# Cosine attention, Fourier mixing and a feed-forward layer on one core: pairs of tiles that cross batches, scoring groups of three, and a new table of priorities

## The chip, the cores and the metric

The kernel runs on one core of one Trainium2 chip. The metric is the device time of one execution in microseconds (us), as the median of the runs shown. The core has five engines with an instruction stream each: TensorE (PE, matmuls; its weight loads are listed apart as PEld), VectorE (DVE), ScalarE (ACT), GpSimd (POOL) and SyncE (SP, which issues most DMAs).

## What is computed

Eight batches, 12 heads, 448 positions, head size 64; D = 768. Inputs and output are float32.

```python
q_n = q / (norm(q) + 1e-6);  k_n = k / (norm(k) + 1e-6)
attn = softmax(q_n @ k_n.T / tau)          # tau = 0.1
x = attn @ v                               # heads side by side: (8, 448, 768)
u = x + real(fft(fft(x, axis=1), axis=2))
un = (u - mean(u)) / sqrt(var(u) + 1e-6)   # over the 768 features
out = u + relu(un @ w_ch1) @ w_ch2         # 768 -> 3072 -> 768
```

## The kernel before

**Stages.** Each batch passes through three. `attn` (line 907) normalizes queries and keys on ACT, DVE and POOL, transposes them by DMA on SP, scores them on PE (line 973 for the three full key tiles of 128, line 986 for the 64 keys that are left, called the tail), takes exponentials on ACT (line 951) and multiplies with the values on PE (lines 1004 and 1010). It does so for six head pairs, called positions. `fft` (line 1165) makes the two transforms as matmuls with cosine and sine matrices; the last of them, over columns, are line 1191. DVE then adds the parts (line 1222), forms u (line 1233) and takes the mean (line 1270). ACT takes the variance and 1/sqrt (lines 1275 and 1278), DVE writes the normalized tile (line 1282, `un`), and SP transposes it by DMA into the buffer UNT (line 1303, `tru`). `ffn` (line 1558) runs the two feed-forward layers.

**Tiles of rows.** The 448 rows of two batches are seven tiles of 128: an even batch has three, an odd one four. A feed-forward unit is one tile or a pair. Which are pairs is set by `units` (line 1322) and by the loop in `ffn` (line 1601): a batch with three tiles has one pair and one lone tile, the lone tile first in batches 0 and 6 and last in 2 and 4; a batch with four has two pairs.

**First layer** (`up`, matmul at line 1350): 24 blocks of 128 hidden features, 6 matmuls each, 144 in all, with 256 columns for a pair and 128 for a lone tile. Pairs of batches 6 and 7 use `ups` (line 1445), a scheme with fewer products that needs sums of weights (DVE, lines 1387 to 1430). The weights of the first layer are in W1b.

**Second layer** (`prod`, matmul at line 1494, always 12 to a product, 384 columns): a lone tile takes 4 products on the weights W2b. A pair takes 7 products by Strassen's scheme: the hidden tiles in the buffer HQ are combined by DVE (`comb`, line 1593: 6 combinations, 3 of them of a third of the length), some products use precomputed sums of weights in the buffer TX, and three products are copied out by ACT (line 1514) and completed by POOL (line 1519). `fin` (lines 1508 to 1530) adds u and `store` (line 1535) writes the rows out.

**Scoring.** PSUM has two pools of buffers, 2 single banks ("M", for feed-forward) and 3 double banks ("G", for scores, values and transforms). One key tile of one position fills a double bank. Which key tiles are scored in one go is the list `steps` (line 958): batch 0 one at a time, batches 1 to 3 two at a time, batches 4 to 7 three at a time:

```python
elif b >= 4:
    steps = [[(pos, kt) for kt in range(3)]]
else:
    steps = [[(pos, 0), (pos, 1)], [(pos, 2), (pos + 1, 0)]] if pos % 2 == 0 else [[(pos, 1), (pos, 2)]]
```

In batches 4 to 7 each key tile of a head is scored by two matmuls (of 128 and 97 columns) per half of the queries, in batches up to 3 by one of 225.

**What sets the order of the work.** The program is a list of operations with inputs, buffers and a priority. A planner (line 257) simulates the five engines with a table of durations and, at each engine, issues the ready operation with the lowest priority number; the result is a fixed instruction order per engine. Second and first layers have priority numbers of 5000 and more, so that they fill what attention and transforms leave free. The table SHIFT (line 80) adds a number to the priority of single operations by name. Where the planner still sees PE idle, filler matmuls are put in (line 1737).

Of the kernel before, what the change touches and what calls it, by code (L numbers as in the profile page):

```python
# [25 lines left out]
TF = 4  # L26
ORDER = (0, 1, 2, 3, 5, 4)
# [473 lines left out]
class Kern:  # L501
# [405 lines left out]
    def attn(self, b):  # L907
# [890 lines left out]
```

## Time and profile before

| | |
|---|---|
| median of 3 runs | 578.84 us (578.64 to 579.3) |
| span of the profiled execution | 575.2 us |
| busy: PE, DVE, ACT, POOL | 97%, 75%, 67%, 38% of the span |
| DMA | 62.20 MB, mean 108 GB/s |
| granted TensorE clock | 9 tenths or more in all 40 slices |

The span is the time from the first to the last instruction that the profiler recorded in one execution; the time of a run is taken outside it and is longer by what lies around the span. The page gives the span of the profiled execution and no other time of it. Busy time is a sum over instructions of one engine. In timelines the matmuls of a run overlap by the depth of PE's pipeline, so a row's length is a little more than the distance from its start to the start of the next row.

### The profile page before, as it was taken

The numbers are of one execution on the slowest core, as the hardware profiler recorded it, in microseconds if no ns is written. First come the engines' busy times: TensorE is split into PE (matmuls) and PEld (weight loads), VectorE is DVE, ScalarE is ACT, GpSimd is POOL, SyncE is SP. The second block draws the span as 40 slices with busy tenths as digits, with TensorE's granted clock in tenths as the row PEclk, the third lists the DMA queues.
The fourth block names the chain that finished last, engine by engine and source line by source line (L and its number), as shares of the span: only waits on it lengthen the run. The fifth ranks groups of instructions, "written<-read, shape, count | busy, mean of one in ns | idle before, by whom it ended". The sixth has DMA issues, their size and how long they took to land.

```text
span 575.2 us, 16313 instructions
## 1 busy us (share of the span) xinstructions
PE 555.8 (97%) x6766; PEld 436.2 (76%) x6766; DVE 430.6 (75%) x917; ACT 385.3 (67%) x724; POOL 220.3 (38%) x332
## 2 busy tenths in 40 slices
PE   3899999999999999999999999999999999989997
PEld 3569787676787686878788787778778787959694
DVE  8989968996669869975669669776778579986262
ACT  7898885564876885687558875577637853747270
POOL 7534414356329544612370724523270210041303
PEclk9999999999999999999999999999999999999999
DMA  9999999975459739952595429743591210023001
GB/s 188 224 233 171 166 186 130 171 152 111 111 94 103 178 76 135 142 127 62 112 121 93 102 80 147 150 84 85 89 113 29 43 57 28 2 43 72 28 28 56
DMA packets 187898, 62.20 MB, mean 108 GB/s; under 512 B 166800, under 2 KB 185616, under 8 KB 187824
## 3 DMA queue, kind: packets, MB, share of 16 engines
q1 hardware_dynamic: 129856, 38.35, 33.7%
q0 software_dynamic: 57968, 22.81, 30.9%
q8 instruction: 53, 0.87, 0.6%
q14 instruction: 21, 0.17, 0.1%
HBM read 51.90 MB, written 11.01 MB: 109 GB/s over the span
## 4 chain that ended last, share of the span: by engine, by line
PE 60%; DVE 4%; ACT 2%; issue 0%; DVEq 0%; ACTq 0%
PE PS L1494 23%; PE PS L1350 20%; PE PS L1445 6%; PE PS L1010 4%; PE PS L973 3%; DVE U L1233 1%; PE PS L1004 1%; PE PS L986 1%; ACT E L951 1%; DVE ACG L1222 1%; ACT F L1275 1%; PE PS L1134 1%; PE PS L1191 1%; DVE SM L885 1%; DVE HQ L1593 1%
## 5 line engine op out<-in xcount | busy, mean ns | idle before, releaser
L1350 PE MATMUL PS<-UNT,W1b 128*128 128x256 bf16 (+1 forms) x1872 | 186.1, 256 | 1.2 <-DMA UNT<-F 0.6
L1350 PEld LDWEIGHTS PS<-UNT,W1b 128*128 128x128 bf16 x1872 | 155.5, 98 | 20.1 <-issue 2.7
L951 ACT ACTIVATE E<-PS 128x900 bf16<-128x900 f32 (+1 forms) x192 | 148.0, 827 | 19.1 <-PE PS L973 16.6
L1494 PE MATMUL PS<-W2b,HQ 128*128 128x384 bf16 x768 | 133.1, 326 | 0.0
L896 POOL TENSOR_TENSOR QH<-STG,SM 128x256 bf16<-128x256 f32 x126 | 82.3, 679 | 91.9 <-DVE SM L702 73.3
L1494 PEld LDWEIGHTS PS<-W2b,HQ 128*128 128x128 bf16 x768 | 73.3, 98 | 46.2 <-issue 0.7
L1519 POOL TENSOR_TENSOR OUTB<-OUTB,U 128x192 f32<-128x192 f32 x66 | 43.2, 675 | 138.5 <-ACT OUTB L1514 137.3
L1366 ACT ACTIVATE HQ<-PS 128x512 bf16<-128x512 f32 x81 | 48.2, 595 | 40.0 <-PE PS L1350 39.5
L1494 PE MATMUL PS<-TX,HQ 128*128 128x384 bf16 (+2 forms) x408 | 69.7, 321 | 1.8 <-ACT MV L1278 1.6
L883 ACT ACTIVATE QH<-STG 128x384 f32<-128x384 f32 x84 | 42.7, 520 | 25.8 <-DVE SM L885 21.3
L1494 PEld LDWEIGHTS PS<-TX,HQ 128*128 128x128 bf16 x408 | 38.4, 98 | 25.7 <-ACT MV L1278 2.0
L1593 DVE TENSOR_TENSOR HQ<-HQ 128x1536 bf16<-128x1536 bf16 (+1 forms) x69 | 49.5, 721 | 9.9 <-ACT HQ L1366 7.1
L885 DVE TENSOR_REDUCE SM<-QH 128x6 f32<-128x384 f32 x84 | 44.7, 544 | 11.3 <-ACT QH L883 11.0
L1010 PE MATMUL PS<-VB,E 128*128 128x65 bf16 x1152 | 51.4, 193 | 0.0
L1366 DVE TENSOR_SCALAR HQ<-PS 128x512 bf16<-128x512 f32 x45 | 31.0, 688 | 23.8 <-PE PS L1350 23.4
L1010 PEld LDWEIGHTS PS<-VB,E 128*128 128x128 bf16 x1152 | 47.7, 97 | 1.2
L1552 POOL DMA_INDIRECT out_dram<-OUTB,IDX x21 | 23.8, 1134 | 56.9 <-DVE OUTB L1530 51.7
L1004 PE MATMUL PS<-VZ,E 128*128 128x130 bf16 x192 | 41.6, 219 | 0.5 <-ACT E L951 0.2
L973 PE MATMUL PS<-QK 64*128 64x225 bf16 (+2 forms) x864 | 39.6, 227 | 0.1
L1233 DVE SCALAR_TENSOR_TENSOR U<-ACG,X 128x768 bf16<-128x768 f32 (+4 forms) x39 | 39.1, 1015 | 0.8
L1530 DVE TENSOR_TENSOR OUTB<-PS,OUTB 128x384 f32<-128x384 f32 x33 | 18.2, 553 | 25.7 <-PE PS L1494 21.9
L1514 ACT ACTIVATE OUTB<-PS 128x384 f32<-128x384 f32 x33 | 16.1, 488 | 29.5 <-PE PS L1494 29.1
(191 smaller groups left out, 793.6 us busy)
## 6 DMA issues: line engine op xcount, KB each, us to landing
STG<-in_q_dram SPq DMA_DIRECT2D x18, 384.0 KB, 4.0
STG<-in_k_dram SPq DMA_DIRECT2D x18, 384.0 KB, 3.8
VB<-in_v_dram POOLq DMA_DIRECT2D x24, 192.0 KB, 7.1
W1b<-in_moe_w_ch_dram POOLq DMA_DIRECT2D x12, 384.0 KB, 7.7
W2b<-in_moe_w_ch_dram POOLq DMA_DIRECT2D x12, 384.0 KB, 7.2
out_dram<-OUTB SPq DMA_DIRECT2D x7, 384.0 KB, 3.4
W2b<-in_q_dram SPq DMA_DIRECT2D x2, 576.0 KB, 10.0
W2b<-in_k_dram SPq DMA_DIRECT2D x2, 576.0 KB, 10.7
```

The costliest lines, as they stand in the source:

```text
L885: P.add("dve", lambda v, o=SS[:, i, H // ns * x:H // ns * (x + 1)], sq=sq: v.tensor_reduce(o, sq.rearrange("p (h d) -> p h d", d=DH), AX.X ...
L896: r = v.tensor_tensor(v3(qh)[:, h:h + 4], v3(buf)[:, h:h + 4], RN[:, i, h:h + 4].unsqueeze(2).to_broadcast((128, 4, DH)), AluOp.mult)
L951: return a.activation(o, self.PS[:, bk:bk + nc_, 0:SQ2], ACTF.Exp, scale=1.0 / self.tau)
L973: i = pe.matmul(self.PS[:, bk + h, c0:c0 + n], self.KT[r, jj, kt * 128:(kt + 1) * 128], self.QT[r, jj, cols], start=True, stop=True)
L1004: r = pe.matmul(o, st(6), self.VZ[:, j, :], start=not split, stop=(split and i == 0), skip_group_check=True)
L1010: r = pe.matmul(o[:, 65 * h:65 * h + 65], st(2 * kt + h), self.VB[:, kt, 2 * j + h, :], start=(split and i == h == kt == 0), stop=((not sp ...
L1233: self.snu.append(P.add("dve", lambda v: v.scalar_tensor_tensor(two(U[o0:o0 + n, ut, :]), src, 1.0, two(X[i0:i0 + n, x, :]), AluOp.mult, A ...
L1350: r = pe.matmul(self.PS[:, bk, x * n:(x + 1) * n], self.W1b[:, j, ft * 128:(ft + 1) * 128], self.UNT[:, j, cs], start=(j == 0), stop=(j == ...
L1366: return e.activation(o, i, ACTF.Relu) if e is self.nc.scalar else e.tensor_relu(o, i)
L1494: r = pe.matmul(self.PS[:, bk, 0:n], lhs(f), rhs(f), start=(start and f == 0), stop=(stop and f == NF // 2 - 1), skip_group_check=True)
L1519: r = g.tensor_tensor(self.OUTB[:, ob, xs], self.OUTB[:, ob, xs], self.U[:, ut, xs], AluOp.add)
L1593: P.add("dve", lambda v: v.tensor_tensor(cs(o), cs(a), cs(bq), op), 0.16 + 0.3 * len(ks), -0.5, f"{nm}{ks[0]}_{b}", reads=rd, writes=[x fo ...
```

## The change

- **Pairs across batches.** `units` now walks through all tiles in order and pairs them, except the two in ONES: the first tile of batch 0 and the last of batch 2 stay alone. Batch 4's last tile (4,2) is paired with batch 5's first (5,0); (5,1) with (5,2); (5,3) with batch 6's first (6,0). `ffn(b)` runs the units whose last tile belongs to b, so (4,2) is now fed forward in batch 5's part, and (5,3) in batch 6's. `up`, `fin` and `store` take the batch of each tile.
- **A tile normalized late.** The last tile of batch 5 (HELD) is not written to UN in `fft`; `unheld`, called after the first layer's matmuls are listed, writes it to a buffer of the QH ring and transposes it from there.
- **Scoring.** Batches 2 and 3 score three key tiles per group. The first scoring group of a batch is also ordered behind the last column transform of the batch before.
- **The end.** The operation `finz` of the last pair also writes OUT1 as a whole, which orders it behind the store that reads OUT1.
- **Priorities.** SHIFT is replaced. It had some 300 entries and has an entry for most operations; two of the rows are shown.

```diff
+ONES = ((0, 0), (2, 2))
+HELD = (5, 3)
...
-    "iotad": {0: 76.7149}, "tpd": {1: 15.2941}, "ktd0": {0: 169.0303}, "ix3": {0: -59.6164}, "ix4": {0: 735.3976}, "vz1": {0: 116.8365},
...
+    "iota": {0: -1027.4994}, "cst": {0: -817.5516}, "iotad": {0: -421.5743}, "rown": {0: -4498.1262}, "tqd": {0: -505.6438, 1: -537.5322},
...
-            elif b >= 4:
+            elif b >= 2:
                 steps = [[(pos, kt) for kt in range(3)]]
...
-                      tiles=new, acquire=new, margin=0.3, order=([self.last_qk] if self.last_qk else []) + self.pvs[-2:-1])
+                      tiles=new, acquire=new, margin=0.3, order=([self.last_qk] if self.last_qk else []) + self.pvs[-2:-1] + (self.fd_ops[-1:] if b and pos == 0 else []))
...
+            if (b, ui) == HELD:
+                self.held = (ut, rn, lp, slot, col)
+                continue
...
+    def unheld(self):
+
+        P = self.P
+        ut, rn, lp, slot, col = self.held
+        b, ui = HELD
+        r = self.qh_next % 6
+        self.qh_next += 1
+        qn = [f"QH{r}"] + ["QH1x"] * (r == 1) + ["QH4x"] * (r in (3, 4))
+        P.add("dve", lambda v: v.tensor_scalar(self.QH[:, r, :], self.U[:, ut, 0:DM], self.MV[:, ut, 0:1], self.RS[:, ut:ut + 1], AluOp.add, AluOp.mult),
+              t_dve(DM, 4) + 0.16, lp, f"un{ui}_{b}", reads=rn + [f"MV{ut}", f"RS{ut}"], writes=qn)
+        self.last_tru = P.add("sp", lambda sy, sem: sy.dma_start_transpose(self.UNT[:, :, col:col + 128], self.QH[:, r, :]).then_inc(sem, 16),
+                              1.45, lp, f"tru{ui}_{b}", reads=[f"QH{r}"], writes=[f"uT{slot}" + x for x in ("", "x", "y")], dma=(f"uT{slot}", 16), serve=1.3)
...
-        self.slots, u = [], 0
-        for b in range(self.nb):
-            sl = []
-            for n in (1, 2) if b in (0, self.nb - 2) else (2, 2) if b % 2 else (2, 1):
-                sl += [2 * (u % 2) + x for x in range(n)]
-                u += 1
-            self.slots.append(sl)
+        self.slots = [[0] * len(self.tiles(b)) for b in range(self.nb)]
+        order = [(b, i) for b in range(self.nb) for i in range(len(self.tiles(b)))]
+        u = x = 0
+        self.pairs = []
+        while x < len(order):
+            n = 1 if order[x] in ONES else 2
+            for y in range(n):
+                b, i = order[x + y]
+                self.slots[b][i] = 2 * (u % 2) + y
+            self.pairs.append(order[x:x + n])
+            u, x = u + 1, x + n
...
-        for i, two in ((0, 0), (1, 1)) if b == self.nb - 2 else [(i, i + 1 < len(tiles)) for i in range(0, len(tiles), 2)]:
+        for k, unit in enumerate([u for u in self.pairs if u[-1][0] == b]):
+            two = len(unit) == 2
+            i = k if b == self.nb - 2 else 2 * k
+            lone = last_b and k == 1
+            b0, u0 = unit[0][0], self.tiles(unit[0][0])[unit[0][1]]
...
-                    self.up(b, (i, i + 1), chunks, True)
+                    self.up(b, unit, chunks, True)
+                    if unit[1][0] == HELD[0] and unit[0][0] < b:
+                        self.unheld()
...
-                                f"finz_{b}", reads=self.unames(b, u1), writes=["OUT1z"], after=(m7,), tiles=(b1,))
+                                f"finz_{b}", reads=self.unames(b, u1), writes=["OUT1z", "OUT1"], after=(m7,), tiles=(b1,))
```

**How the instructions move.** The rows are the instruction order of one engine, with line, operation, buffers and count; a line of "..." stands for the other value groups. The line numbers of the changed kernel differ (973 is now 1385, 986 is 1398, 1004 and 1010 are 1416 and 1422, 1222 is 1634, 1350 is 1782, 1494 is 1926, 1593 is 2026).

First place, PE in the scoring of batch 2, positions 0 to 2, between feed-forward products of batch 1. Before:

```order
L973 MATMUL PS<-QK 128x225 x8
L1494 MATMUL PS<-W2b,HQ 128x384 x12
L973 MATMUL PS<-QK 128x225 x8
L986 MATMUL PS<-QK,KTD 128x225 x2
L1494 MATMUL PS<-W2b,HQ 128x384 x4
L1494 MATMUL PS<-TX,HQ 128x384 x8
L1004 MATMUL PS<-VZ,E 128x130
L1010 MATMUL PS<-VB,E 128x65 x6
...
L973 MATMUL PS<-QK 128x225 x8
```

Now, from one group of three to the next:

```order
L1385 MATMUL PS<-QK 128x225 x12
L1926 MATMUL PS<-W2b,HQ 128x384 x8
L1416 MATMUL PS<-VZ,E 128x130
L1422 MATMUL PS<-VB,E 128x65 x6
...
L1398 MATMUL PS<-QK,KTD 128x225 x2
L1926 MATMUL PS<-W2b,HQ 128x384 x8
L1385 MATMUL PS<-QK 128x225 x12
```

Three groups of 8 have become two groups of 12, and the work between two groups has become 16 product matmuls, four value groups and a tail.

Second place, PE after batch 5's column transform (the line with CS,E). Before:

```order
L1191 MATMUL PS<-CS,E 128x2x96
L1494 MATMUL PS<-W2b,HQ 128x384 x20
L1494 MATMUL PS<-TX,HQ 128x384 x12
L1350 MATMUL PS<-UNT,W1b 128x128 x72
```

Now:

```order
L1603 MATMUL PS<-CS,E 128x2x96
L1926 MATMUL PS<-W2b,HQ 128x384 x8
L1926 MATMUL PS<-TX,HQ 128x384 x24
L1926 MATMUL PS<-W2b,HQ 128x384 x24
L1926 MATMUL PS<-TX,HQ 128x384 x12
L1782 MATMUL PS<-UNT,W1b 128x256 x12
```

The first layer behind the products was that of the lone tile (4,2) and is that of the pair (4,2) and (5,0). DVE now, from the first sum of batch 5's last transform to the normalization of the tile (5,0), which is the last row:

```order
L1634 TENSOR_TENSOR ACG<-PS,ACG 128x388 x2
L1963 TENSOR_TENSOR OUTB<-PS,OUTB 128x384
L2026 TENSOR_TENSOR HQ<-HQ 128x1536
L1645 SCALAR_TENSOR_TENSOR U,ACG<-ACG,X 128x768
L1682 TENSOR_SCALAR MV<-ACG 128x1
L1645 SCALAR_TENSOR_TENSOR U,ACG<-ACG,X 128x768
L1634 TENSOR_TENSOR ACG<-PS,ACG 128x388 x2
L1297 TENSOR_REDUCE SM<-QH 128x6
L1697 TENSOR_SCALAR F<-U,MV 128x768
```

These are 9 rows; before, 24 rows stood from that sum to that normalization.

Third place, DVE around the last transform (batch 7), where combinations of batch 6's pair (HQ<-HQ) stand between sums, u and means of batch 7. Before:

```order
L1222 TENSOR_TENSOR ACG<-PS,ACG 128x388 x2
L1593 TENSOR_TENSOR HQ<-HQ 128x512
L1465 TENSOR_TENSOR HQ<-PS,E 128x384
L1233 SCALAR_TENSOR_TENSOR U,ACG<-ACG,X 97x768
L1593 TENSOR_TENSOR HQ<-HQ 128x512
L1253 COPY ACG<-ACG 1x2
L1253 COPY U<-U 1x768
L1593 TENSOR_TENSOR HQ<-HQ 128x1536
L1270 TENSOR_SCALAR MV<-ACG 128x1
L1593 TENSOR_TENSOR HQ<-HQ 128x1536
```

Now:

```order
L1897 TENSOR_TENSOR HQ<-PS,E 128x384 x2
L1895 TENSOR_SCALAR HQ<-PS 128x384
L2026 TENSOR_TENSOR HQ<-HQ 128x512 x2
L1645 SCALAR_TENSOR_TENSOR U,ACG<-ACG,X 128x768
L2026 TENSOR_TENSOR HQ<-HQ 128x1536
L1634 TENSOR_TENSOR ACG<-PS,ACG 128x388
L2026 TENSOR_TENSOR HQ<-HQ 128x1536
```

The update of 97 rows, the two copies of one row and the mean now stand behind the second long combination.

## Rows read from the trace of the kernel before

**Rows 1.** the page, part 1: busy time, share of the span and instructions of each engine

```profile
PE 555.8 (97%) x6766; PEld 436.2 (76%) x6766; DVE 430.6 (75%) x917; ACT 385.3 (67%) x724; POOL 220.3 (38%) x332
```

**Rows 2.** stretches: start:end, length, busy us (instructions) of PE, PEld, DVE, ACT, POOL; PEclk, DMA, GB/s

```profile
0.00:46.00 46.00, 33.54 (x488) 26.02 (x489) 40.83 (x94) 39.60 (x61) 26.22 (x57) 1.00 1.30 212
...
46.00:500.00 454.00, 452.21 (x5501) 356.19 (x5500) 348.10 (x743) 311.15 (x596) 174.77 (x244) 1.00 0.67 108
...
340.00:420.00 80.00, 79.92 (x1014) 63.51 (x1013) 58.42 (x125) 51.46 (x98) 30.85 (x46) 1.00 0.65 104
...
500.00:520.00 20.00, 18.36 (x170) 12.70 (x167) 15.99 (x37) 10.85 (x28) 7.04 (x8) 1.00 0.33 64
```

**Rows 3.** waits of PE: line that waits, what it waits for, total us, times, longest

```profile
PE PS L1494 <- ACT MV L1278: 1.6, 1, 1.6
```

**Rows 4.** timeline of PE, 180 to 215 us: start, us, instruction, count

```profile
182.11 4.07 PE L1494 MATMUL PS<-TX,HQ 128*128 128x384 bf16 x24
...
186.01 1.46 PE L1494 MATMUL PS<-W2b,HQ 128*128 128x384 bf16 x8
...
187.41 0.56 PE L973 MATMUL PS<-QK 64*128 64x225 bf16 x8
...
187.90 2.77 PE L1494 MATMUL PS<-W2b,HQ 128*128 128x384 bf16 x16
...
194.85 4.76 PE L1350 MATMUL PS<-UNT,W1b 128*128 128x256 bf16 x42
...
199.54 0.56 PE L973 MATMUL PS<-QK 64*128 64x225 bf16 x8
```

**Rows 5.** timeline, 462 to 520 us, the lone tile of batch 6

```profile
471.11 5.86 PE L1350 MATMUL PS<-UNT,W1b 128*128 128x128 bf16 x102
...
476.80 7.96 PE L1494 MATMUL PS<-W2b,HQ 128*128 128x384 bf16 x48
```

**Rows 6.** timeline of PE, 449 to 482 us: two scoring groups of batch 7

```profile
456.80 0.78 PE L973 MATMUL PS<-QK 64*128 64x128 bf16 x24
...
457.51 1.48 PE L1494 MATMUL PS<-W2b,HQ 128*128 128x384 bf16 x8
...
459.97 1.46 PE L1494 MATMUL PS<-W2b,HQ 128*128 128x384 bf16 x8
...
461.36 0.78 PE L973 MATMUL PS<-QK 64*128 64x128 bf16 x24
```

**Rows 7.** groups by form: the score exponentials, and operations that a pair adds

```profile
L951 ACT ACTIVATE E<-PS 128x900 bf16<-128x900 f32 x144 | 124.6, 920 | 17.1 <-PE PS L973 16.6
...
L1593 DVE TENSOR_TENSOR HQ<-HQ 128x1536 bf16<-128x1536 bf16 x36 | 35.6, 988 | 2.4 <-PE PS L1494 1.6 <-DVE MV L1270 0.4
...
L1514 ACT ACTIVATE OUTB<-PS 128x384 f32<-128x384 f32 x33 | 16.1, 488 | 29.5 <-PE PS L1494 29.1
...
L1519 POOL TENSOR_TENSOR OUTB<-OUTB,U 128x192 f32<-128x192 f32 x66 | 43.2, 675 | 138.5 <-ACT OUTB L1514 137.3 <-POOL QK L920 0.2
```

**Rows 8.** transform to normalized tile, batches 2 and 5: last column-transform matmul, first UNT transpose

```profile
182.02 0.25 PE L1191 MATMUL PS<-CS,E 65*128 65x192 bf16 x1
...
190.06 3.23 SPq L1303 DMA_TRANSPOSE UNT<-F  x2
...
363.13 0.25 PE L1191 MATMUL PS<-CS,E 65*128 65x192 bf16 x1
...
379.10 5.21 SPq L1303 DMA_TRANSPOSE UNT<-F  x4
```

**Rows 9.** DMA issues: what, engine, count, median us to landing

```profile
UNT<-F SPq DMA_TRANSPOSE x25, 2.8
```

**Rows 10.** timeline, 500 to 507 us, last transform: DVE and PE

```profile
503.48 1.28 DVE L1593 TENSOR_TENSOR HQ<-HQ 128x1536 bf16<-128x1536 bf16 x1
...
505.22 0.96 DVE L1593 TENSOR_TENSOR HQ<-HQ 128x1536 bf16<-128x1536 bf16 x1 [0.39 <-DVE MV L1270]
...
506.32 0.97 PE L1494 MATMUL PS<-TX,HQ 128*128 128x384 bf16 x5 [1.64 <-ACT MV L1278]
```

More of the change, by code (lines that the diff above doesn't have):

```diff
@@ L1337, in up @@
         P = self.P
-        sl = [self.slots[b][i] for i in idx]
+        sl = [self.slots[x][i] for x, i in idx]
         n = 128 * len(sl)
@@ L1531, in fin @@
         on = f"OUT{ob}" + "b" * c + "z" * (c0 > 0)
-        return self.P.add("dve", fn, t_dve(c1 - c0), -1, f"{nm}_{b}", reads=([on] if src == "out" else self.unames(b, ut)) + [f"RS{ut}"] * late, writes=[on],
+        return self.P.add("dve", fn, t_dve(c1 - c0), -1, f"{nm}_{b}", reads=([on] if src == "out" else self.unames(bt, ut)) + [f"RS{ut}"] * late, writes=[on],
                           after=(op,), tiles=(tile,))
@@ L1562, in ffn @@
         if b == 0:
-            self.up(0, (0,), range(0, NF, 4), False)
-            self.up(0, (1, 2), range(0, NF, 2), True)
+            self.up(0, ((0, 0),), range(0, NF, 4), False)
+            self.up(0, ((0, 1), (0, 2)), range(0, NF, 2), True)
             for i, ut in enumerate(tiles):
@@ L1614, in ffn @@
                 op = self.prod(b, b1, H(0), W(0, 0), hr(0), wr(0), f"m1{i}", True, False)
-                rd = self.fin(b, b1, op, 0, 0, u0, "a", f"fa{i}")
+                rd = self.fin(b, b1, op, 0, 0, u0, "a", f"fa{i}", bt=b0)
                 comb(0, 4, 0, range(3), AluOp.subtract, "s2")
                 op = self.prod(b, ta, H(1), W(1, 0), hr(1), wr(1), f"m2{i}", True, True)
-                self.fin(b, ta, op, 0, 0, u0, "out", f"fin{i}0")
-                if last_b and i + 2 == len(tiles):
-                    self.store(b, i, u0, 0, 0)
+                self.fin(b, ta, op, 0, 0, u0, "out", f"fin{i}0", bt=b0)
+                if lone:
+                    self.store(b0, i, u0, 0, 0)
                 comb(1, 1, 0, range(3), AluOp.subtract, "s4")
                 op = self.prod(b, b1, H(0), TT(1), hr(0), tr(2), f"m6{i}", False, False, rd)
-                rd = self.fin(b, b1, op, 0, 1, u0, "a", f"fv{i}")
+                rd = self.fin(b, b1, op, 0, 1, u0, "a", f"fv{i}", bt=b0)
                 op = self.prod(b, tb, H(4), TT(0), hr(4), tr(1), f"m5{i}", True, False)
@@ L1628, in ffn @@
                 rd = self.fin(b, b1, op, 1, 1, u1, "out", f"fin{i + 1}1")
-                if last_b and i + 2 == len(tiles):
+                if lone:
                     self.store(b, i + 1, u1, 1, 1)
                 op = self.prod(b, tb, H(1), W(1, 1), hr(1), wr(1), f"m3{i}", False, True, rd2)
-                self.fin(b, tb, op, 0, 1, u0, "out", f"fin{i}1")
-                self.store(b, i, u0, 0, 1 if last_b and i + 2 == len(tiles) else None)
-                if last_b and i + 2 == len(tiles):
+                self.fin(b, tb, op, 0, 1, u0, "out", f"fin{i}1", bt=b0)
+                self.store(b0, i, u0, 0, 1 if lone else None)
+                if lone:
                     tz, cz = Tile("G"), slice(256, 384)
                     pre = P.add("dve", lambda v: v.tensor_tensor(self.OUTB[:, 1, cz], self.PS[:, self.bank(b1), cz], self.U[:, u1, cz], AluOp.add), t_dve(128), -1,
-                                f"finz_{b}", reads=self.unames(b, u1), writes=["OUT1z"], after=(m7,), tiles=(b1,))
+                                f"finz_{b}", reads=self.unames(b, u1), writes=["OUT1z", "OUT1"], after=(m7,), tiles=(b1,))
                     op = self.prod(b, b1, H(3), lambda f: self.TX[:, 2, f, 0:256], hr(3), tr(4), f"m4{i}", False, True, rd, n=256, more=[pre])
@@ L1649, in ffn @@
                 continue
-            u0 = tiles[i]
-            self.up(b, (i,), (0, 12, 4, 16, 8, 20), False)
+            self.up(b, unit, (0, 12, 4, 16, 8, 20), False)
             comb(4, 0, 2, range(3), AluOp.add, "s5")
@@ L1657, in ffn @@
                 op = self.prod(b, tile, H(q1), r1, hr(q1), w1, f"{n1}{i}", False, True)
-                self.fin(b, tile, op, 0, c, u0, "u", f"fin{i}{c}")
-            self.store(b, i, u0, 0)
+                self.fin(b, tile, op, 0, c, u0, "u", f"fin{i}{c}", bt=b0)
+            self.store(b0, i, u0, 0)
     def sums(self, done):
```

19 lines of the change are left out of this document (11 added, 8 removed), and 526 rows, old and new, of the table SHIFT.

## The prediction, made before the changed kernel was run

> **What bounds the kernel now.** I read first the page's busy shares, then the stretches, then PE's waits, then its timeline. TensorE (PE) is busy 97% of the span and no other engine passes 75% [rows 1]. A busy share is an average, so the stretches come next: in the first 46 us PE works 33.5 us and waits for the others, from 46 to 500 us it works 452.2 of 454.0 us, and from 500 to 520 us it works 18.4 [rows 2]. The waits say the same: past the start one wait of 1.6 us stands out, where line 1494 waits in the feed-forward part of batch 6 [rows 3]; the timeline puts it near 506 us [rows 10]. So between 46 us and the end a matmul removed is time removed, unless the work that hides the other engines gets too thin. The granted clock is 1.00 of full speed in all four stretches [rows 2], so a matmul has one price throughout: 2.4 GHz.
>
> Prices are distances from start to start, since the lengths in the rows overlap. 24 second-layer matmuls of 384 columns take 186.01 - 182.11 = 3.90 us, 0.1625 each; the next 8 should take 1.30 and take 1.40, because a scoring group follows: **entering** the scoring group's 64-row form costs 0.10. The group of 8 takes 187.90 - 187.41 = 0.49 [rows 4]. 42 first-layer matmuls of 256 columns take 4.69 less the 0.10, so 0.1093 each [rows 4]; 102 of 128 columns (a lone tile) take 5.69, so 0.0558 each [rows 5].
>
> **The change, part by part.** 1. Two lone tiles become one pair. Second layer: two lone tiles are 2 x 48 matmuls, a pair 7 products x 12 = 84, so 12 x 0.1625 = **-1.95 us**, all on PE's path. First layer: 2 x 144 x 0.0558 = 16.07 against 144 x 0.1093 = 15.74, **-0.33 us**. The first layer gains little because the row shows the 128-column matmul at half the price of the 256-column one. The Trainium skill (TensorE: Matmul & The Clock Gate, Back-to-back issue gap) says instead that in a stream of weight loads and matmuls a 128-column matmul takes about 81 ns; an estimate from that page makes the lone tiles 288 x 0.081 = 23.3 us, and this term about -7.6 us. The row decides: 102 in a row at 56 ns.
>
> The pair costs the other engines: per pair 6 combinations in place of 2 on DVE (3 long ones at 0.99 us and 3 of a third of the length against 2 long ones: some 2 us more, at most 4 x 0.99 = 4.0), 3 copies on ACT (3 x 0.49 = 1.5) and 6 additions on POOL (6 x 0.675 = 4.1) [rows 7]. In the 80 us around the two places PE works 79.9, DVE 58.4, ACT 51.5 and POOL 30.9 us [rows 2]. They fit beside PE: 0. Should the cover go, the first 4.0 us of it would show.
>
> 2. Batches 2 and 3 score three key tiles per group: 6 groups per batch in place of 9, of 12 matmuls in place of 8. Before, a batch pays 9 x (0.49 + 0.10) = 5.31. A group of 12 is not in the trace. From below: 4 more matmuls run in pairs, so they stream 450 columns more, at the 0.42 ns per column of the long streams 0.19, so 0.68. From above: half as much again as 8, 0.735. The nearest row is the group of 24 of batches 4 to 7, which streams the same columns in shorter pieces: 457.51 - 456.80 = 0.71 [rows 6]. I take 0.69: 6 x 0.79 = 4.74, so -0.57 per batch, **-1.15 us** (ends -0.6 and -1.3).
> Does the larger group starve ACT or PE? It needs all three double banks at once, so scoring and exponentials take turns. Batches 4 to 7 do it already: in batch 7 two groups start 461.36 - 456.80 = 4.56 us apart, with 8 matmuls of 384, four value groups, the tail scores and 8 more of 384 between them [rows 6], in a stretch without a PE wait. The new order of batch 2 has, at its tightest, the same work between two groups (the first place of the order); elsewhere in batches 2 and 3 it is as much or more. That is the spacing that worked. 0.
>
> 3. Batch 4's last tile waits for batch 5's first, and the pair's first layer is the next work after 68 matmuls of 384 columns behind batch 5's column transform: 68 x 0.1625 = **11.05 us of cover** (the second place of the order). Within it the tile must be summed, normalized and transposed. The trace has this path in two lengths: in batch 2 the first transpose is issued 190.06 - 182.27 = 7.8 us after the last transform matmul, in batch 5 379.10 - 363.38 = 15.7, where nobody was in a hurry [rows 8]. A transpose lands after 2.8 [rows 9]. So 10.6 or 18.5 us against 11.05: a wait of 0 to 7.5. I take 0, as the new VectorE (DVE) order puts 9 rows between the transform and this tile's normalization where 24 stood. Late next, with no slack left, is that tile.
>
> 4. Batch 5's last tile is normalized late into a QH buffer. One DVE operation and one transpose on SP move; none is added. On SP one load of batch 7 (k, third tile) stands behind that transpose, and its use comes after more than 30 us of PE's work (the 84 second-layer matmuls of the first pair and the 144 first-layer matmuls of the next are 13.7 + 15.7): 0. On POOL two stores change places with nothing urgent behind them. The last correction before the end now also waits for a store of the preceding pair, which is a whole first layer of 252 matmuls older: 0. The scoring of a batch is ordered behind the last transform of the batch before: an order that PE has anyway.
>
> 5. New priorities. In the last transform, PE stands 1.64 us because the combination that feeds it ends at 506.18, after one of 1.28 us and a gap of 0.39 on DVE [rows 10]. In the new order an addition, an update of 97 rows, two copies and a mean (the third place) no longer stand ahead of it. PE arrives no later, so I take half the wait off, **-0.8** (ends -1.64, and +1.5 if the wait doubles). In the first 46 us ACT idles 6.4 and DVE 5.2 us [rows 2]; there the order differs in swaps of neighbours and one absolute value that goes from ACT to DVE. **-0.3** (ends -1 and +1). For new short waits elsewhere, where PE stood only 1.8 us in 454 [rows 2], **+0.4** (ends 0 and +2). The 6 filler matmuls on W1b that go stood in a wait: 0.
>
> **Sum:** -1.95 - 0.33 - 1.15 - 0.8 - 0.3 + 0.4 = -4.1. The profiled execution spans 575.2 us, so 571.1; the median of the runs, 578.84, has 3.6 us around the span: **574.7 us**.
>
> **The rivals.** A. Waits all vanish: the removed 3.4 plus the whole 1.64, 1 at the start and 1 of the 1.8 in the middle, 571.8. For it: DVE's order near the end. Against: every order so far kept some.
> B. The gain is half eaten: new priorities open waits of 3.6 us, twice the 1.8 that stand there now, in the long middle that PE has less work to fill (one tile less during batch 5's attention): 578.3, no change. For it: ACT and DVE are 70 to 77% busy there, so a chain can be late; against it: 1.8 us of waits in 454.
> C. Slower: at the pair of batches 4 and 5 the tile takes batch 5's old path, 18.5 us, against 11.05 of cover [rows 8, 9]: PE stands 7.5 us, 574.7 + 7.5 = 582.2. It turns from a loss of nothing above 11.05 us and makes the whole change a loss above some 15.2. For it: this chain has only 0.5 us of slack by batch 2's length; against it: the new DVE order has been cleared ahead of it.
> D. The groups of three starve. A group, three exponentials and at most a fourth for the tail, one after the other, take 0.69 + 4 x 0.92 = 4.4 us on ACT [rows 7]; with two 0.49 copies of another stage between, 5.4, against 4.56. Then the 5 distances of batch 2 grow by up to 0.8 and those of batch 3 by some 0.2: 5.0 in all, 579.7; with one copy 4.9, 5 x 0.3 = 1.5, 576.2. Against it: the same spacing runs without a wait [rows 6]. The Trainium skill (TensorEngine Tiling (Array Packing), PSUM Bottleneck) warns of this: tiling speeds TensorE, not the copies out of PSUM. The trace of batch 7 does not show it.
> E. The removed 128-column matmuls cost a weight load each. At the average of all weight loads, 436.2 / 6766 = 0.064 us [rows 1], 288 of them are worth 288 x 0.0086 = 2.5 us more, 572.2. Against: 102 in a row at 0.056 [rows 5]. The page on the issue gap, above, leans that way.
>
> **How the numbers follow.** My forecast 0.75, A 0.08, E 0.02, B and D together 0.09, C 0.06. A measurement of this kernel tells 0.2% (1.2 us) from no change, so faster is below 577.7: forecast, A and E, 0.85; B and D stand mostly within 0.2%, 0.08, and a little of them with C slower, 0.07. The range goes from A, 571.8, with no more than the ends below it left out, to the forecast with no help from the priorities (+0.8 and +0.3), +1 at the start and 1.3 of new waits, 578.1.
>
> **What would show it.** 420 and 720 second-layer matmuls on TX and W2b in place of 384 and 768; scoring groups of 12 at about 0.69 us; no wait of the first first-layer matmul behind batch 5's transform; the wait near the end under 1 us; PE busy over 99% from 46 to 500 us. Wrong would be: a wait of PE on a UNT transpose of microseconds (C), waits of ACT's exponentials passed on to PE in batches 2 and 3 (D), or a start that is later by more than 1 us.

## The result and the profile after

| | before | the change |
|---|---|---|
| median (lowest to highest) of 20 runs, us | 578.70 (577.54 to 579.97) | 580.51 (578.01 to 583.49) |
| ratio to before, with its 95% interval | | 1.0034 (1.0022 to 1.0046) |
| span of the profiled execution, us | 575.2 | 581.6 |

The change is slower by 0.34%, 1.8 us on the medians, where 4.1 us of gain were forecast; the time lies above the range. The profiled execution of the change is the slowest of its 20, 583.49 us, so its trace shows more waits than a middling run has. Its time is 1.9 us longer than its span, and that of the other runs 1.8 to 1.9. The execution of before in the trace, with its span of 575.2, then took some 577.1 us, 1.6 under the median. (The prediction took 3.6 us for what lies around the span; 1.7 of it was the distance of that execution from the median.) So the spans of the two traces lie 6.4 us apart where the medians lie 1.8 apart, and what follows from the two traces is too large by some 4.6 us in all.

Part 1 of the page of the change [rows 1]:

```profile
PE 556.3 (96%) x6592; PEld 434.1 (75%) x6592; DVE 434.7 (75%) x917; ACT 386.7 (66%) x731; POOL 234.1 (40%) x338
```

174 matmuls are gone from the rows (fillers among them), yet PE is busy as long as before. POOL is busy 13.8 us longer.

Stretches of the change, with the columns of [rows 2]:

```profile
0.00:46.00 46.00, 33.45 (x457) 25.39 (x458) 39.92 (x89) 37.75 (x60) 25.64 (x55) 1.00 1.34 207
...
46.00:500.00 454.00, 444.89 (x5222) 347.10 (x5222) 346.64 (x733) 308.64 (x593) 189.22 (x251) 1.00 0.69 109
...
340.00:420.00 80.00, 76.63 (x901) 58.82 (x900) 62.45 (x132) 49.87 (x95) 37.18 (x49) 0.98 0.76 110
...
478.00:490.00 12.00, 10.36 (x74) 6.02 (x72) 10.99 (x15) 1.47 (x3) 7.18 (x6) 1.00 0.00 0
...
500.00:520.00 20.00, 19.77 (x220) 15.06 (x218) 17.60 (x38) 13.47 (x32) 4.99 (x6) 1.00 0.10 19
```

From 46 to 500 us PE now works 444.9 of 454.0 us; before it worked 452.2 [rows 2]. So 7.3 us of idle time came into the stretch that had 1.8. In the 80 us around the two crossing pairs (340 to 420 us) it works 76.6 where it worked 79.9. Near the end (500 to 520 us) it works 1.4 us more than before: the wait of [rows 10] is gone.

Waits of PE in the change (the last of three columns is the longest):

```profile
PE PS L1782 <- ACT HQ L1798: 2.9, 2, 2.2
...
PE PS L1926 <- DVE OUTB L1963: 2.3, 3, 1.8
...
PE PS L1416 <- issue: 1.0, 1, 1.0
```

None of the three stood in [rows 3]. To balance the account, the timelines of PE give the start of the first feed-forward matmul and that of PE's last run of 24 matmuls. Before:

```profile
48.46 4.72 PE L1350 MATMUL PS<-UNT,W1b 128*128 128x128 bf16 x77
...
569.56 2.14 PE L1494 MATMUL PS<-TX,HQ 128*128 128x256 bf16 x24
```

In the change:

```profile
50.68 2.50 PE L1782 MATMUL PS<-UNT,W1b 128*128 128x128 bf16 x42 [0.19 <-ACT CS L2124]
...
576.35 2.14 PE L1926 MATMUL PS<-TX,HQ 128*128 128x256 bf16 x24
```

The stretch between these two rows, less the gaps that PE's timeline shows in it, is PE's working time:

| us | before | change | difference |
|---|---|---|---|
| start of the first feed-forward matmul | 48.5 | 50.7 | +2.2 |
| gaps of PE behind it | 3.4 | 9.0 | +5.6 |
| working time | 517.7 | 516.7 | -1.0 |
| start of the last run of matmuls | 569.6 | 576.4 | +6.8 |

The forecast for these three was -0.3, -0.4 (-0.8 and +0.4) and -3.4. The first two failed by 8.5 us together in this trace; the third is 2.4 short, of which some 1.7 is a stretch at a lower clock, below. By the medians the whole miss is 5.9 us (1.8 of loss and 4.1 of gain that did not come) and not 10.9.

**The longest wait.** ACT and PE around 352 us, timeline of the change:

```profile
352.83 0.52 ACT L1295 ACTIVATE QH<-STG 128x384 f32<-128x384 f32 x1 [2.74 <-DMA QK<-QH]
...
353.38 0.52 ACT L2124 ACTIVATE KTD<-QK 64x384 bf16<-64x384 bf16 x1
...
353.92 0.60 ACT L1798 ACTIVATE HQ<-PS 128x512 bf16<-128x512 f32 x1
...
354.57 2.71 PE L1782 MATMUL PS<-UNT,W1b 128*128 128x256 bf16 x12 [2.19 <-ACT HQ L1798]
```

ACT takes its list in order. The relu (line 1798) that hands PE its next hidden block stands behind a square of batch 6's queries (line 1295), which stands 2.74 us until a transpose that reads its buffer has landed. PE then waits 2.19 us. The 12 matmuls behind it take 2.71 us, 0.226 each, where 256 columns cost 0.109 [rows 4]. The stretch behind the wait:

```profile
354.30:358.00 3.70, 3.43 (x17) 2.46 (x18) 2.81 (x8) 2.34 (x6) 1.49 (x3) 0.55 1.40 111
```

The granted clock is 0.55 of full, near the lower of the two levels (1.2 of 2.4 GHz). At 0.109 the 12 would have taken 1.31, and with the five matmuls behind them the stretch lost some 1.7 us.

**The second.** DVE, POOL and PE from 482 us on, the second product stage of the crossing pair (5,3) and (6,0):

```profile
482.46 2.01 POOL L1952 TENSOR_TENSOR OUTB<-OUTB,U 128x192 f32<-128x192 f32 x2 [1.15 <-ACT OUTB L1947]
...
482.75 1.30 DVE L2026 TENSOR_TENSOR HQ<-HQ 128x1536 bf16<-128x1536 bf16 x1
...
483.98 1.30 DVE L1819 TENSOR_TENSOR STG<-W1b 128x1536 bf16<-128x1536 bf16 x1
...
485.30 2.48 POOL L1952 TENSOR_TENSOR OUTB<-OUTB,U 128x192 f32<-128x192 f32 x2 [0.83 <-ACT OUTB L1947]
...
488.51 0.94 DVE L1819 TENSOR_TENSOR QH<-STG,W1b 128x1536 bf16<-128x1536 bf16 x1
...
489.71 0.55 DVE L1963 TENSOR_TENSOR OUTB<-PS,OUTB 128x384 f32<-128x384 f32 x1
...
490.32 1.96 PE L1926 MATMUL PS<-TX,HQ 128*128 128x384 bf16 x11 [1.79 <-DVE OUTB L1963]
```

POOL's last additions for this correction are through at 485.30 + 2.48 = 487.8. The correction (line 1963) that takes them over stands on DVE behind weight sums (line 1819) and others and starts at 489.71. PE waits 1.79 us.

**The start.** The first feed-forward matmul starts at 50.68 and not 48.46. That is more than the 1 us by which the prediction said it would be wrong. The fillers of the first 14 us, in the change and then before:

```profile
12.84 1.49 PE L2175 MATMUL PS<-TX 128*128 128x128 bf16 x12
...
14.12 0.85 PE L1232 MATMUL PS<-TX,QH 128*128 128x128 bf16 x3
```

```profile
12.63 0.50 PE L1737 MATMUL PS<-TX 128*128 128x128 bf16 x6
...
13.71 0.83 PE L1737 MATMUL PS<-TX 128*128 128x128 bf16 x12
```

At 12.8 us 12 fillers (matmuls that only keep PE busy) stand in the change where 6 stood before, and they take 1.49 us; the 12 of before took 0.83. From start to start that is 14.12 - 12.84 = 1.28, 0.107 each, twice the 0.0558 of [rows 5]. The trace's record of the granted clock begins at 16.7 us in the change and at 11.2 us before, at full speed in both. Ahead of its first entry a stretch is printed with 1.00, so that figure says nothing about 12.8 us; the half pace says that PE was most likely at its lower level there, and the record that it came to the full one 5.5 us later than before.

### The profile page after: what moved, and what is told of

It reads as the page before. It is cut to its first block, busy times and chain, and to the rows that moved or that the text cites. A ratio compares the mean times of both kernels' runs of the same rounds, so it can differ in the third digit from the quotient of the medians.

```text
span 581.6 us, 15988 instructions
## 1 busy us (share of the span) xinstructions
PE 556.3 (96%) x6592; PEld 434.1 (75%) x6592; DVE 434.7 (75%) x917; ACT 386.7 (66%) x731; POOL 234.1 (40%) x338
## 5 line engine op out<-in xcount | busy, mean ns | idle before, releaser
L1926 PE MATMUL PS<-W2b,HQ 128*128 128x384 bf16 x720 | 125.5, 326 | 0.4 <-ACT OUTB L1947 0.4
L1308 POOL TENSOR_TENSOR QH<-STG,SM 128x256 bf16<-128x256 f32 x126 | 87.5, 720 | 76.1 <-DVE SM L1114 57.1
L1952 POOL TENSOR_TENSOR OUTB<-OUTB,U 128x192 f32<-128x192 f32 x72 | 51.6, 737 | 129.1 <-ACT OUTB L1947 128.1
L1926 PEld LDWEIGHTS PS<-W2b,HQ 128*128 128x128 bf16 x720 | 68.4, 98 | 43.8 <-DVE F L1697 0.6
L1926 PE MATMUL PS<-TX,HQ 128*128 128x384 bf16 (+2 forms) x444 | 76.5, 322 | 2.4 <-DVE OUTB L1963 2.3
L1798 ACT ACTIVATE HQ<-PS 128x512 bf16<-128x512 f32 x85 | 50.4, 594 | 31.5 <-PE PS L1782 30.5
L1926 PEld LDWEIGHTS PS<-TX,HQ 128*128 128x128 bf16 x444 | 41.7, 98 | 29.1 <-DVE OUTB L1963 3.4
L2026 DVE TENSOR_TENSOR HQ<-HQ 128x1536 bf16<-128x1536 bf16 (+1 forms) x73 | 53.0, 729 | 13.7 <-ACT HQ L1798 7.9
L1295 ACT ACTIVATE QH<-STG 128x384 f32<-128x384 f32 x84 | 43.2, 520 | 22.3 <-DVE SM L1297 14.5
L1422 PE MATMUL PS<-VB,E 128*128 128x65 bf16 x1152 | 51.6, 193 | 0.0
L1798 DVE TENSOR_SCALAR HQ<-PS 128x512 bf16<-128x512 f32 x41 | 28.3, 690 | 26.3 <-PE PS L1782 25.8
L1687 ACT ACTIVATE F<-U,MV 128x768 bf16<-128x768 bf16 x28 | 26.0, 930 | 14.5 <-DVE MV L1682 10.9
```

The source lines that it names most:

```text
L1295: P.add("act", lambda a, sq=sq, src=buf[:, w * x:w * x + w]: a.activation(sq, src, ACTF.Square), t_act(w), pr, f"sq{i}_{b}", reads=bn, wri ...
L1308: r = v.tensor_tensor(v3(qh)[:, h:h + 4], v3(buf)[:, h:h + 4], RN[:, i, h:h + 4].unsqueeze(2).to_broadcast((128, 4, DH)), AluOp.mult)
L1422: r = pe.matmul(o[:, 65 * h:65 * h + 65], st(2 * kt + h), self.VB[:, kt, 2 * j + h, :], start=(split and i == h == kt == 0), stop=((not sp ...
L1798: return e.activation(o, i, ACTF.Relu) if e is self.nc.scalar else e.tensor_relu(o, i)
L1926: r = pe.matmul(self.PS[:, bk, 0:n], lhs(f), rhs(f), start=(start and f == 0), stop=(stop and f == NF // 2 - 1), skip_group_check=True)
L1952: r = g.tensor_tensor(self.OUTB[:, ob, xs], self.OUTB[:, ob, xs], self.U[:, ut, xs], AluOp.add)
```

## The experiments

Fifteen runs follow, in four groups; two of them repeat a kernel as it is. Ratios are to the kernel before, run beside each on the same chip, with 95% intervals; times are medians. Each trace is of one execution.

**1. The change once more, and its single waits.** Is it these waits that cost the time, each to be cured by an edit of the order, or does the time go elsewhere when one is cured? First the change as it is.

> The changed kernel unchanged, for a second trace. Theory W (the removed matmuls are gone as forecast and the orders put waits on TensorE in their place): the same waits stand again, 2 us before batch 4's first layer near 352 us with the matmuls behind it at half pace, 0.7 near 418, 1.8 near 488, 1.0 near 195, and 2 us at the start; 580.5 against 578.7 of before. Rival N (the profiled run was the slowest of 20, so its waits are its own): most of these waits are under 0.5 us in the new trace, other places have taken their turn, and the median is again 580 to 581.

Measured: 581.50 us (5 runs), 1.0050 (1.0037 to 1.0063). Waits of PE in its trace:

```profile
PE PS L1926 <- DVE OUTB L1963: 2.3, 3, 1.8
...
PE PS L1926 <- DVE HQ L2026: 1.6, 1, 1.6
...
PE PS L1782 <- DMA UNT<-F: 1.5, 1, 1.5
...
PE PS L1782 <- ACT HQ L1798: 0.5, 1, 0.5
```

```profile
50.26 2.95 PE L1782 MATMUL PS<-UNT,W1b 128*128 128x128 bf16 x50 [0.19 <-DVE UNT L1715]
...
574.70 2.14 PE L1926 MATMUL PS<-TX,HQ 128*128 128x256 bf16 x24
```

The wait for line 1963 (1.79 us again) and the one of 1.0 in batch 3 recur. The wait of 2.19 us on the relu is 0.5 here, and two others stand instead: 1.6 us on a combination (no such wait stands in the first trace) and 1.5 us on the transposes of the tile (5,0). The granted clock from 350 to 360 us is 1.00. The start is 50.26, the gaps behind it add up to 9.3 us, and 574.70 - 50.26 - 9.3 leaves 515.1 us of working time, 2.6 less than before. So part of the waits move from one execution to the next, and in these two their sum stays.

Three edits of the fixed order, each alone. The relu and its neighbours are moved on ACT ahead of the squares that wait:

```diff
+        self.put('act', 'relu8_4', ('sq6_6', 0))
+        self.put('act', 'relu20_4', ('sq6_6', 0))
+        self.put('act', ('relu0_5', 1), ('sq6_7', 0))
```

> Three relu copies on ScalarE (batch 4's eighth and twentieth block, batch 5's first of its second pair) go ahead of the squares and the query copy that wait for a transpose. Theory W: the wait near 352 us and the half-pace matmuls behind it go, 2.2 + 1.7, and the 0.7 near 418: in the trace 3 to 4.6 us less in these two places, the median 577 to 578.5. Rival N: the median stays within 0.7 us of the changed kernel's.

Measured: 582.53 us (5 runs), 1.0070 (1.0057 to 1.0083).

```profile
PE PS L1926 <- DVE OUTB L1963: 2.3, 3, 1.8
...
PE PS L1546 <- DVE F L1510: 2.0, 2, 1.1
...
PE PS L1926 <- ACT HQ L1798: 1.5, 1, 1.5
```

The relu is early, and waits of 1.5 (a later relu) and of 1.1 and 0.9 (the row transform) stand further on. The gaps sum to 9.95 us. So the place of this relu is not what costs the time. That the squares which were passed delay others, and that the chain of ACT, DVE and DMA as a whole is late here, fits the new waits but was not tested.

The correction of the second wait is put on DVE right behind the operation T31_6, ahead of the weight sum:

```diff
+        self.put('dve', 'fin11_6', 'T31_6', True)
```

> One correction on VectorE (second tile of the pair of batches 5 and 6, upper half) goes ahead of an attention product and a sum of weights. Theory W: the wait of 1.8 us near 488 falls to under 0.5 and the median is 1 to 1.5 us lower than the changed kernel's. Rival N: within 0.7 us of it. Rival L (the longer VectorE operations beside GpSimd's additions are the bound there, whatever their order): the wait moves behind the next sum of weights and stays over 1 us.

Measured: 580.61 us (12 runs), 1.0038 (1.0022 to 1.0054).

```profile
PE PS L1782 <- DMA UNT<-F: 1.5, 1, 1.5
...
PE PS L1926 <- DVE HQ L2026: 0.7, 1, 0.7
...
PE PS L1877 <- ACT E L1886: 0.6, 1, 0.6
...
PE PS L1926 <- DVE OUTB L1963: 0.5, 2, 0.3
```

The waits for line 1963 fall from 2.3 to 0.5 us, as the edit meant. The median stays near the change's (it is 0.9 us under that of the repeat above, with intervals that overlap): DVE is busy 13.0 of the 14 us from 478 to 492, a wait of 0.6 on ACT stands at 491, and 0.7 on a combination near 183 and 1.5 us on the tile (5,0) stand here too. Then the 12 fillers at 12.84 us, removed:

```diff
+        at = [op.name for op in pe].index("tk0_0") + 1
+        while pe[at].name == "warm":
+            pe.pop(at)
```

> The 12 filler matmuls between the first key transposes and the first query transposes are taken out. Theory W (fillers at half pace, 1.49 us, stand ahead of the query transposes whose inputs are there): the first scoring group starts 1 to 1.3 us earlier, the first feed-forward matmul 1 us or more, and the median is some 1 us lower. Rival N: the start is the same to 0.3 us because something else, a load or GpSimd, is late there. Rival C (fewer fillers keep TensorE at its lower level longer): the start is later by up to 2 us.

Measured: 580.41 us (12 runs), 1.0028 (1.0016 to 1.0040); the first feed-forward matmul starts at 51.61. Four traces with these fillers (the change, again, relu, fin) have it at 50.18 to 51.48, so it starts no sooner without them: the slow fillers are not what delays the start. The clock record begins at 18.6 us here and at 16.7 in the change, which is what rival C expected; one trace doesn't settle it.

**2. The same structure with other priorities.** Here the table of the change is replaced by one found by a search over plans of the kernel's own planner, with every DMA taken 0.3 us later and POOL 5% longer than the planner has them. The search was made four times: for the whole change, for the pairs without the groups of three, for the groups of three without the pairs, and for the structure of before. If the structure costs the time, the first stays slow.

```diff
-SHIFT = {
+PRIO = {
...
-            op.prio = round(op.prio + SHIFT.get(op.name, {}).get(k, 0), 4)
+            op.prio = PRIO[op.name][k]
```

> The change with a third table of priorities, searched anew so that the order also stands when each DMA lands 0.3 us later and GpSimd takes 5% longer. Theory O (the pairs and groups give what their matmuls say, and the change's own table of priorities gives it back): the first feed-forward matmul stands before 49 us, the waits behind it sum to under 7 us against 9 to 10, and the median is 576 to 578, below before's 578.5. Rival S (the structure makes the waits: the pair of batches 4 and 5 ends in the transform's chain, the pair of 5 and 6 puts GpSimd's additions beside the sums of weights): 579 or more, with 2 us or more of waits in each of these two stretches again.

Measured: **575.92 us** (5 runs), 0.9943 (0.9927 to 0.9958): faster than both kernels, by 3.0 us than the one before.

```profile
46.00:500.00 454.00, 449.40 (x5345) 353.92 (x5343) 348.84 (x740) 315.82 (x605) 183.39 (x251) 1.00 0.70 108
...
478.00:490.00 12.00, 11.48 (x117) 8.21 (x116) 12.00 (x23) 3.91 (x9) 3.24 (x4) 1.00 0.17 67
```

```profile
50.76 2.45 PE L1654 MATMUL PS<-UNT,W1b 128*128 128x128 bf16 x41
...
569.12 2.14 PE L1798 MATMUL PS<-TX,HQ 128*128 128x256 bf16 x24
```

PE works 449.4 of the 454 us, and 11.48 of 12 in the stretch where the correction was late (its two waits for corrections of that pair, at 477 and 484 us, are 0.39 and 0.45). The gaps behind the first feed-forward matmul are 4.5 us, and 569.12 - 50.76 - 4.5 leaves 513.9 us of working time, 3.8 less than before. The start is as late as in the change.

The parts alone. Pairs without the groups of three:

```diff
-            elif b >= 2:
+            elif b >= 4:
```

> The pairs across batches without the groups of three in batches 2 and 3, priorities searched in the same way. By the matmuls 1.15 us slower than the kernel with both (t_again). Theory O: 577 to 579. Rival S: 580 or more, as the stretches of the two pairs are the same. Rival G (the groups of three cost waits that eat their 1.15 us, as the 1.0 us at 195 us suggests): the same as t_again or faster.

Measured: 578.15 us (11 runs), 0.9989 (0.9978 to 1.0000). Groups of three on the kernel before, with the order of `finz` that the change gives it:

```diff
-            elif b >= 4:
+            elif b >= 2:
...
-                                f"finz_{b}", reads=self.unames(b, u1), writes=["OUT1z"], after=(m7,), tiles=(b1,))
+                                f"finz_{b}", reads=self.unames(b, u1), writes=["OUT1z", "OUT1"], after=(m7,), tiles=(b1,))
```

> The groups of three without the pairs across batches, priorities searched in the same way. Theory O: 2.3 us slower than the kernel with both, 578 to 580, and 1.15 faster than t_same. Rival S: faster than t_again, 577 to 578, without waits over 1 us between 300 and 375 us. Rival G: no faster than t_same, with waits of value matmuls on exponentials of about 1 us in batches 2 and 3.

Measured: 582.76 us (5 runs), 1.0062 (1.0047 to 1.0076), with 6.9 us of gaps. The structure of before with priorities searched in the same way:

> The kernel before with priorities searched in the same way: what the search alone is worth. Theory O and Rival G: 577 to 579, no more than 1.5 us off before's 578.5. Rival S: the fastest or second of the four.

Measured: 579.06 us (11 runs), 1.0000 (0.9984 to 1.0017). Its traced execution, the slowest of the 11 at 583.08, has 6.8 us of gaps. So the search by itself gave nothing on the old structure, and with the whole new one 3 us. How the gain divides between pairs and groups of three this doesn't settle: the groups cost 3.7 us on the structure of before and gain 2.2 on the pairs, while all that differs elsewhere is a table each. The terms are smaller than what one table differs from the next.

**3. The start.** The 279 operations that stand ahead of the first feed-forward matmul are given the order that the kernel before has, and the rest of the change is kept; the scheduler takes the order from a list:

```diff
+                    if left_in[e][-1] != op.key:
+                        continue
```

> The change with the order of the kernel before for everything that was planned ahead of the first feed-forward matmul (60 operations on TensorE, 63 on ScalarE, 97 on VectorE, 44 on GpSimd, 15 on SyncE); the rest in the change's own order. Theory O, its first part (the new order of the start costs 1.8 to 3 us): the first feed-forward matmul stands near 48.2 us as in before's trace, and the median falls by 1.5 to 2.5 us, to 578 to 579. Rival N (the start's time differs from run to run whatever the order, 48 to 52 us in the traces so far): 50 us again, and the median stays at 580 to 581.

Measured: 578.26 us (12 runs), 0.9991 (0.9975 to 1.0008). By the ratios that is 0.43%, 2.5 us, less than the change. The first feed-forward matmul starts at 49.73, and the gaps behind it are 7.3. PE's order up to 17 us is that of before, row for row, yet it starts 1.3 us later than in before's trace: the clock record begins at 16.4 us and not at 11.2, and the 12 fillers of before's row at 13.71 take 1.47 us here and took 0.83. So part of the late start is the clock of the execution and not the order. The same start ahead of the order that did best:

> The same start in front of the searched order (t_again). Theory O: the first feed-forward matmul near 48.2 in place of 50.5, and 573.5 to 575 against 575.9. Rival N: 575.5 to 577, no gain.

Measured: 577.01 us (12 runs), 0.9975 (0.9966 to 0.9984), first feed-forward matmul at 49.79. It starts 1.0 us sooner than the fastest kernel and is 1.1 slower on the medians, 1.9 by the ratios. The gaps of its trace are 6.8 us and not 4.5, but this execution is its slowest, 578.59. So the sooner start brought nothing here; that the order behind it could not use it is likely and not shown. For scale, the kernel before once more in one execution:

> The kernel before, unchanged, for a second trace. Theory O: the first feed-forward matmul near 48.2 us again (within 0.5), and waits behind it of 3 to 4.5 us. Rival N: the start is 1 us or more off the first trace's.

Measured: 577.71 us, first feed-forward matmul at 48.77.

```profile
46.00:500.00 454.00, 451.96 (x5493) 355.97 (x5491) 347.86 (x743) 310.53 (x595) 175.09 (x244) 1.00 0.66 108
```

Its traces agree within 0.3 us in this stretch (452.21 and 451.96), and those of the change within 0.1.

**4. Slack or luck.** Was the allowance for late DMAs what made the searched order good, or is one draw as good as another? Four further searches for the whole structure: n1 and n2 for the shortest plan, r3 and r4 with the allowance. The edit is that of the second group.

> The change's structure with priorities searched for the shortest plan alone, without any allowance for late DMAs or a slower GpSimd. Theory K (the gain of t_again comes from the slack that its search asked for): 578 to 581, waits behind the first feed-forward matmul of 7 us or more, as in the change. Rival D (t_again was a lucky draw; orders differ by a few us on the chip whatever the search asked for): no pattern between the two kinds, each anywhere from 575 to 581. Rival P (any better plan is better on the chip): the shorter plan is the faster, so this one is at or below t_again's 575.9.

> The same search, for the shortest plan alone, from another random start. Theory K: 578 to 581 again. Rival D: anywhere from 575 to 581, at least 2 us off n1. Rival P: at or below 575.9.

> The search with slack of t_again from another random start. Theory K: 574.5 to 577, waits behind the first feed-forward matmul of 4 to 6 us. Rival D: anywhere from 575 to 581. Rival P: slower than n1 and n2, 577 or more.

> The search with slack, a third random start. Theory K: 574.5 to 577 again, so that both are faster than n1 and n2. Rival D: anywhere from 575 to 581. Rival P: 577 or more.

| | runs | median, us | ratio (95%) | gaps behind the first feed-forward matmul, us |
|---|---|---|---|---|
| n1 | 12 | 577.94 | 0.9995 (0.9983 to 1.0007) | 5.6 |
| n2 | 11 | 577.65 | 0.9996 (0.9978 to 1.0013) | 2.8 |
| r3 | 11 | 577.64 | 0.9990 (0.9979 to 1.0001) | 3.9 |
| r4 | 9 | 576.17 | 0.9970 (0.9951 to 0.9989) | 2.8 |

Each count of gaps is of one execution: that of n1 ran 1.1 us under its median, those of n2 and r4 1.8 us, that of r3 at it. With the allowance the three medians are 575.9, 577.6 and 576.2, without it 577.9 and 577.7. That leans towards slack, but one of the three lies with the other two, so it stays open. What the five show together: every one is faster than the change's 580.5, two of them are faster than before beyond their intervals, and none is slower than before.

## Why the prediction was wrong

**What failed is step 5**, the new priorities, in two of its terms. "-0.3" for the start (ends -1 and +1) measured +2.2 and +1.8: I read the swaps in the order and saw none that cost anything, and looked at no chain through them. Giving back the old order of the start brought 2.5 us by the ratios, of which the start itself is 0.5 to 1.0 in the traces and part is the clock's (group 3). And "+0.4" for new short waits (ends 0 and +2) measured +6.7 and +7.0 where the two traces' +5.6 and +5.9 are cleared of the 1.1 that the last transform gained. By the medians, which lie closer than the traces, step 5 as a whole missed by some 5.5 us: 1.8 of loss, where some 3 of work went, leaves 4.8 of cost for the order, and -0.7 was forecast (-0.8, -0.3 and +0.4). I took the 1.8 us of waits that stood before as a property of the kernel. It was a property of the old table: t_same, another table on that structure, left PE idle for 6.2 of the 454 us in its slowest execution. The five searched tables on the structure of the change have gaps of 2.8 to 5.6 us, the change's 9.0 and 9.3, and all five are faster than it. Which chain in the change's table each wait goes back to stays open: no edit of a single place behind the start brought the time back.

**Steps 1 and 2, the work removed, were right in kind.** The counts are those forecast (by form, in the change):

```profile
L1926 PE MATMUL PS<-W2b,HQ 128*128 128x384 bf16 x720 | 125.5, 326 | 0.4 <-ACT OUTB L1947 0.4
...
L1926 PE MATMUL PS<-TX,HQ 128*128 128x384 bf16 x420 | 74.4, 326 | 2.4 <-DVE OUTB L1963 2.3
```

PE's working time fell by 2.6 us in the second trace of the change, and by 3.8 in the best searched order (3.2 to 4.2 over all five); 3.4 was forecast. A group of 12 costs 140.34 - 139.65 = 0.69 us, and two groups start 149.08 - 144.54 = 4.54 apart without a wait between, the 4.56 of [rows 6]:

```profile
139.65 0.76 PE L1385 MATMUL PS<-QK 64*128 64x225 bf16 x12
...
140.34 2.77 PE L1926 MATMUL PS<-TX,HQ 128*128 128x384 bf16 x16
...
144.54 0.76 PE L1385 MATMUL PS<-QK 64*128 64x225 bf16 x12
...
149.08 0.76 PE L1385 MATMUL PS<-QK 64*128 64x225 bf16 x12
```

So rival D, groups of three that starve, fell at this spacing. It came true at one place, the first value matmuls of batch 3, here in the change and in t_again:

```profile
195.69 0.22 PE L1416 MATMUL PS<-VZ,E 128*128 128x130 bf16 x1 [0.96 <-issue]
...
194.52 0.23 PE L1288 MATMUL PS<-VZ,E 128*128 128x130 bf16 x1 [0.66 <-ACT E L1235]
```

Four exponentials stand in a row on ACT there (2.96 us), and PE has 12 matmuls of 384 columns and a tail (some 2.2 us) to do meanwhile. Every trace of the whole structure has this wait, 0.66 to 1.32 us, about what the groups were forecast to bring in both batches (1.15); t_pairs has none, and t_groups, with 16 matmuls of 384 in that place, has none either. Rival E fell too: with its 2.5 us PE's working time would have fallen by 5.9, and it fell by 4.2 at most (r4). By the figure of the Trainium skill (TensorE: Matmul & The Clock Gate, Back-to-back issue gap) the first layer alone would have given 7.6 us; no run shows a working time that is shorter by that much. Rival A, without any wait, was not seen in any order.

**Step 1's cover of 0** for the other engines was too good. POOL's additions and DVE's sums of weights lie together at 478 to 490 us, where POOL had nothing to do before. Before, and then all additions of the change:

```profile
478.00:490.00 12.00, 12.00 (x140) 9.35 (x139) 11.78 (x27) 4.35 (x10) 0.00 (x0) 1.00 0.09 34
...
L1952 POOL TENSOR_TENSOR OUTB<-OUTB,U 128x192 f32<-128x192 f32 x72 | 51.6, 737 | 129.1 <-ACT OUTB L1947 128.1
```

PE lost 1.6 us there. The 6 additions more (72 in place of the 66 of [rows 7]) were priced at 4.1 us; all 72 take 51.6 us where 66 took 43.2, so 8.4 more. The structure does not have to lose it: t_again waits 0.84 us for the corrections of this pair, though additions and weight sums lie together there too, and n1, r3 and r4 show no wait of PE from 478 to 490 us. So most of it is the order's, that is the table's.

**Step 3's 0** for the tile (5,0) held in the first trace of the change (its 0.3 us of wait there is put down to a correction) and is 1.4 to 1.5 us in three others (again, fin, start):

```profile
373.86 1.47 PE L1782 MATMUL PS<-UNT,W1b 128*128 128x256 bf16 x12 [1.47 <-DMA UNT<-F]
```

That is rival C at a fifth of its size, and the sum of step 3 gives it: in again the transpose is issued 8.5 us after the last transform matmul and lands 4.0 us later, 12.5 in all against the 11.05 of cover. In the first trace the two are 7.85 and 2.9, 10.75 in all. So what was mis-sized is mainly the landing, taken at its median of 2.8 us [rows 9], and 0.7 us of the path before it, with only 0.5 us of slack. In t_again the landing is 2.8 again, and a scoring group stands in the cover besides.

**The wait near the end** went as said. The gaps behind the last transform fall from 1.6 to 0.5 us, -1.1 where -0.8 was forecast.

**Rival B** was nearest: new waits of 3.6 us in the long middle. They were 7.3, with a late start on top. The condition I gave it (a chain of ACT and DVE is late) is what the row at 352 us shows. Its chance of 0.09 together with D was set by the 1.8 us of waits that stood before, which were evidence on another table.

## What to carry to other kernels

Price the removed work and the new order apart. Removed matmuls can be read off the trace to a few tenths, but a replaced table of priorities is a term of its own, here worth up to 4.6 us on one structure (575.9 to 580.5), more than all the work removed; before a structure is judged, its order should be drawn more than once. A single wait that is cured by an edit is no gain while the engine behind it is as late with the next thing: look for how much the sum of waits falls.

## What was not expected of the hardware

- **The clock behind a wait.** After a wait of 2.19 us of PE the granted clock was 0.55 over 3.7 us; in fill a wait of 2.23 us at the same place was followed by 3.4 us at the lower level too. After the wait of 1.79 us at 488 us it stayed at 1.00:

```profile
490.00:494.00 4.00, 3.68 (x43) 2.91 (x44) 4.00 (x10) 1.17 (x4) 1.46 (x1) 1.00 0.02 4
```

- **The first microseconds run at either level.** 12 fillers of 128 columns took 1.49 us at 12.84 us and before took 0.83 at 13.71; the clock record begins at 16.7 and at 11.2 us, and matmuls ahead of it run at half pace. In start, with before's order up to there, it begins at 16.4. So the prediction's one price throughout, read from a 1.00 over the first 46 us, doesn't hold in the first 11 to 17 us, nor does the clock of all 40 slices in the table of before hold for the first of them: a 1.00 where nothing is recorded is no reading.
- **DVE beside POOL.** An operation of DVE on 1536 columns takes 0.95 us at most places, and 1.30 in the two rows at 482 to 485 us, beside two additions of POOL that take 2.01 us; the two at 485.30 take 2.48, where the mean would be 2 x 0.675 = 1.35 [rows 7]. The 1.28 us of [rows 10] is of this kind (two additions run from 503.40 to 505.16). But an operation of 0.95 at 479.45 lies beside two additions that take 2.69 from 478.62, so that the two engines slow each other is likely and not shown.
